# Sliding-window attention and a token/channel mixer on one Trainium2 core: one pool of eight PSUM banks, one burst of scores per pair of heads, sinks' values by the whole array

## Chip, cores, metric

The kernel runs on one core of one Trainium2 chip. The metric is the device time of one execution in microseconds (us); lower is better. The engines are named as in the profile: PE (matmuls; PEld are its weight loads), DVE (vector), ACT (scalar and exp), POOL (which here mostly issues DMAs that cast), SP (which issues DMAs).

## The reference

```python
# q, k, v: (4 batches, 8 heads, 768 rows, 64); n_sink = 4, window = 128
scores = (q @ k.T) / 8
keep = (pos_k < 4) | ((pos_q - pos_k >= 0) & (pos_q - pos_k < 128))
a = softmax(where(keep, scores, -1e9))
x = (a @ v)                         # laid out as (4, 768, 512)
h = relu(x.T @ w_tok1) @ w_tok2     # 768 -> 256 -> 768, over the rows
u = x + h.T
out = u + relu(u @ w_ch1) @ w_ch2   # 512 -> 1536 -> 512, over the channels
```

Each query row thus sees the 128 keys up to its own and the first four keys of the sequence, the sinks.

## The kernel before

**Tiles.** The 8 heads of a batch are taken as 4 pairs, 16 pairs in all (0 to 3 are batch 0). Scores are made transposed: keys on the partitions, queries along the free dimension, the two heads `i` of a pair beside each other. A key tile `kt` of 128 keys needs only query tiles `kt` and `kt + 1`, so a pair has six key tiles of 256 queries (128 for the last); two key tiles are a group `g`, and a pair has three groups. ACT takes exp of a group out of PSUM into `pT` (L588). Then either DVE multiplies by a mask of ones and zeros (L596), or, in some groups of batch 0, PE has added -32768 before the scores (`masked`, units named `m` in FIRST_BATCH). `v_aug` is v with a column of ones, so that the value matmuls also give the sum of exps; DVE takes the reciprocal and multiplies (L656 to L700) into `x_sb`.

**Sinks.** Query tiles 2 to 5 see the sinks outside their window. `score_sinks` (L610) takes two pairs at once: four matmuls of 512 columns, 32 rows for each head of each pair, and one exp into `pT_sink`. `v_sink` holds the sinks' values in the matching rows and zeros elsewhere: two copies of four rows for each pair (`sink_rows`, L727). In batch 0 and for pair 15, `pv` (L635) adds them by one whole-array matmul of 130 columns for each query tile. From pair 4 to 14, `sink_values` (L676) does it with eight matmuls of 64 rows, and `values` (L711) follows with eleven whole-array matmuls of 65 columns for each head.

**Order.** All engines run an order that the program works out while it is built: a planner (class `Plan`, L265) with a cost for each operation places units of PE work and hands evictions to ACT or DVE, whichever is sooner. It hands out PSUM banks too: a unit starts on PE only when the banks that it needs have been read. Three lists written out by hand steer it. FIRST_BATCH orders the units of batch 0's attention and token mixer. From then on the channel mixer is the main list: for each batch 24 units `v1` (four matmuls of 384 columns each, relu by ACT or DVE) and then 24 units `out` (three matmuls of 512 columns, four units into one bank). Attention and token mixer of the next batches are the side list, and MERGED says for each side unit after how many main units it is placed. LOADS orders the loads on POOL's queue. Units that use only a part of the array are gathered into a `burst`, since a change between whole-array and partial work costs PE time (SWITCH in the planner).

**PSUM** has eight banks of 128 x 512 fp32: two pairs of banks with the tag `sc` for scores (and the q and k transposes of pairs 5 to 7), four single banks `mx` for the rest. A pair of banks that held transposes is cleared by a memset (L521), because exp reads places that no score was written to, and exp of a stale number times a mask of zero may not be zero.

**A pair from 4 on** has two bursts: the transposes of the next pair's q and k if PE does them (pairs 5 to 7; from pair 8 on DMAs transpose), the scores of group 0 by halves (K = 64, 128 keys), and the sink values of the pair before; then, later, groups 1 and 2 by eighths (32 keys by 160 queries, eight parts of the array side by side), and for every other pair the sinks' scores.

**Start.** SP issues the fp32 loads of q and k of pairs 0 and 1, four small loads of the first batch's sinks into `v_sink_f` (L213) and the loads of pairs 2 and 3. POOL copies `v_sink_f` to `v_sink` (one copy), and then issues v1, v2, w_tok1 (`T0`) and so on.

Of the kernel before, what the change touches and what calls it, by code (L numbers as in the profile page):

```python
# [9 lines left out]
FP32 = mybir.dt.float32  # L10
# [6 lines left out]
def kernel(  # L17
# [35 lines left out]
    )  # L53
    FIRST_BATCH = (
        "q0 k0 m00 s00 m01 s01 q1 m02 k1 s02 m11 x1 s11 m10 q2 s10 o01 m12 k2 s12 o00 m21 q3 s21 s20 k3 o11 "
        "s22 x3 o10 m31 s30 s31 o20 h0 m32 o21 s32 h1 o30 o31 y01 u00 h2 u10 u11 t00 h3 u20 t01 t11 y30 t10 "
        "u21 t20 t30 u31 t31 t21"
    )
    LOADS = (
        "v1 v2 T0 v3 A0 k4 q4 q5 C0 v4 k5 C1 v5 q6 C2 k6 C3 k7 q7 D0 q8 v6 k8 D1 D2 D3 v7 k9 q9 q10 v8 k10 "  # L60
        "k11 q11 v9 v10 k12 k13 q12 q13 v11 v12 k14 q14 v13 k15 q15 v14 v15"
# [16 lines left out]
    TAGS = {"sc": 2, "mx": 4}  # L78

    given = {}  # L80

    sc = [psum.tile([P, 2, 2, 4, D], FP32, name=f"ps_sc{n}", tag=f"sc{n}", bufs=1) for n in range(TAGS["sc"])]

    def bank(tag, *shape, dtype=FP32, slot=None):

        n = given[tag].pop(0) if slot is None else slot
        if tag == "sc":
            return sc[n]
        return psum.tile([P, *shape], dtype, name=f"ps_{tag}", tag=f"{tag}{n}", bufs=1)
# [69 lines left out]

    ones = singles.tile([P, 4 * P], BF16)  # L160
    in_order(nc.vector.memset(ones, 1.0))  # L161

    def keep_warm(n, slot):
        ps = bank("mx", 4 * P, slot=slot)
        for _ in range(n):
            mm(ps, ones[:, 0:P], ones, start=True, stop=True)

    keep_warm(7, 0)


# [4 lines left out]
    MASKED = -32768.0  # L175
    mask_add = singles.tile([P, 4, 2, P], BF16)
# [993 lines left out]
```

## Time and profile before

| | |
|---|---|
| three runs | 199.54, 199.54, 199.82 us; median 199.54 |
| the profiled execution | 199.51 us, of which the span from first to last instruction is 197.7 |
| granted clock of PE | 1.00 throughout |

In a row of the order of time stand the start in us, the length, the engine, the line, the operation, output and input with their shapes, and how many of them in a row were merged; in brackets the idle time before it and what ended it. In a row of the groups stand busy time in all, mean ns of one, and the idle time of the engine before them. Matmuls are pipelined: the length of a row contains the latency of the last one, and the distance of two starts is what PE spent. Nearly all matmuls have the line of a helper, L134, so they are told apart by tiles and shapes: `ps_sc<-qT,kT` are scores, `ps_mx<-qT,kT` sink scores, `ps_mx<-v_sink,pT_sink` sink values, `ps_mx<-v_aug,pT` values, `ps_mx<-uT,w_ch` v1 units and `ps_mx<-w_ch,v1T` out units.

### The profile page before, as it was taken

To read this page: it belongs to the slowest core of one execution; us is meant where nothing else is said; L and a number is where in the kernel's file an instruction comes from. 1 tells how busy PE (TensorE), PEld (TensorE's weight loads), DVE (VectorE), ACT (ScalarE), POOL (GpSimd) and SP (SyncE) were. 2 spreads that over 40 slices of the span, in tenths; PEclk is the share of its full clock that TensorE was granted. 3 is DMA by queue.
4 is the path that set the end of the run, shared out by engine and by line. 5 is a ranking of instruction groups with operands and counts; after the bars stand their busy time and mean duration, and the time that the engine had idled before them with its cause. 6 is when DMAs were issued, how large, how long until landed. Compare 5 with 4: busy or idle time off the path is not lost.

```text
span 197.7 us, 5262 instructions
## 1 busy us (share of the span) xinstructions
PE 190.7 (96%) x2251; PEld 114.5 (58%) x2251; DVE 102.6 (52%) x218; ACT 106.6 (54%) x188; POOL 67.6 (34%) x86
## 2 busy tenths in 40 slices
PE   6798999999999999999999999999999999999993
PEld 1345895566764655565556755566656645564453
DVE  4697775878774656340756886443352631001222
ACT  4798657987717027867735753868701006772000
POOL 6099797789538933159450000000000000000000
PEclk9999999999999999999999999999999999999999
DMA  6999999999999999999999997100002391000223
GB/s 193 281 268 150 169 176 177 188 179 169 183 154 162 133 179 206 156 183 137 148 156 143 209 175 182 56 0 5 0 0 109 84 230 57 0 3 0 106 106 106
DMA packets 92359, 26.30 MB, mean 133 GB/s; under 512 B 82352, under 2 KB 89392, under 8 KB 92336
## 3 DMA queue, kind: packets, MB, share of 16 engines
q0 software_dynamic: 67232, 11.80, 81.5%
q1 hardware_dynamic: 25104, 14.17, 34.6%
q8 instruction: 17, 0.28, 0.6%
q14 instruction: 6, 0.05, 0.1%
HBM read 26.75 MB, written 6.29 MB: 167 GB/s over the span
## 4 chain that ended last, share of the span: by engine, by line
PE 88%; DMA 7%; POOL 1%; DVE 1%; SPq 0%; issue 0%; POOLq 0%
PE ps_mx L134 82%; PE ps_sc L134 4%; DMA w_tok<-in_moe_w_tok_dram 4%; DMA v_sink_f<-in_v_dram 3%; POOL v_aug L127 1%; PE ps_mx L137 1%; PE ps_sc L503 1%; PE ps_mx L475 1%; SPq L213 0%; POOL v_sink L143 0%; PE ps_mx L487 0%; DVE v_sink_f L209 0%; DVE mask_add L178 0%; DVE ones L161 0%; DVE v_aug L195 0%
## 5 line engine op out<-in xcount | busy, mean ns | idle before, releaser
L134 PE MATMUL ps_mx<-w_ch,v1T 128*128 128x512 bf16 (+2 forms) x312 | 67.2, 363 | 0.0
L134 PE MATMUL ps_mx<-uT,w_ch 128*128 128x384 bf16 x384 | 66.8, 326 | 0.0
L147 ACT ACTIVATE v1T<-ps_mx 128x384 bf16<-128x384 f32 x82 | 40.3, 492 | 29.6 <-PE ps_mx L134 18.1
L588 ACT ACTIVATE pT<-ps_sc 128x1024 bf16<-128x1024 f32 (+1 forms) x48 | 44.2, 952 | 16.0 <-PE ps_sc L134 15.7
L134 PEld LDWEIGHTS <-w_ch 128*128 128x128 bf16 x384 | 36.0, 98 | 23.5 <-issue 0.9
L134 PEld LDWEIGHTS <-v1T 128*128 128x128 bf16 x312 | 28.3, 98 | 26.8 <-issue 0.2
L1006 DVE TENSOR_TENSOR o_sb<-ps_mx,u_sb 128x512 f32<-128x512 f32 x23 | 15.9, 690 | 36.9 <-PE ps_mx L134 31.1
L119 POOL DMA_DIRECT2D q_bf<-in_q_dram x24 | 19.8, 830 | 15.2 <-DMA v_aug<-in_v_dram 6.8
L134 PEld LDWEIGHTS <-w_tok 128*128 128x128 bf16 x240 | 19.5, 98 | 5.2 <-issue 0.4
L119 POOL DMA_DIRECT2D k_bf<-in_k_dram x24 | 19.8, 832 | 5.3 <-DMA v_aug<-in_v_dram 2.2
L805 DVE TENSOR_TENSOR u_sb<-ps_mx,x_sb 128x512 bf16<-128x512 f32 (+1 forms) x24 | 15.4, 655 | 8.2 <-PE ps_mx L134 8.0
L127 POOL DMA_DIRECT2D v_aug<-in_v_dram x16 | 16.5, 1038 | 7.3 <-DMA w_ch<-in_moe_w_ch_dram 2.2
L149 DVE TENSOR_SCALAR v1T<-ps_mx 128x384 bf16<-128x384 f32 x14 | 7.6, 550 | 18.9 <-PE ps_mx L134 18.8
L134 PEld LDWEIGHTS <-pT 128*128 128x128 bf16 x352 | 14.7, 98 | 4.0 <-issue 1.0
L134 PE MATMUL ps_mx<-v_aug,pT 128*128 128x65 bf16 x352 | 16.1, 193 | 0.0
L596 DVE TENSOR_TENSOR pT<-pT,mask_main 128x768 bf16<-128x768 bf16 (+1 forms) x25 | 14.8, 617 | 2.0 <-ACT pT L588 1.9
L134 PE MATMUL ps_mx<-h1T,w_tok 128*128 128x256 bf16 (+1 forms) x120 | 14.2, 251 | 0.0
L134 PE MATMUL ps_sc<-qT,kT 64*32 64x160 bf16 (+3 forms) x480 | 14.0, 232 | 0.2 <-ACT kT L141 0.2
L147 ACT ACTIVATE h1T<-ps_mx 128x512 bf16<-128x512 f32 (+1 forms) x9 | 4.5, 505 | 16.1 <-PE ps_mx L134 16.1
L134 PEld LDWEIGHTS <-kT 64*32 64x32 bf16 (+1 forms) x512 | 7.1, 91 | 9.1 <-issue 7.8
L134 PE MATMUL ps_mx<-x_sb,w_tok 128*128 128x256 bf16 (+1 forms) x120 | 12.2, 251 | 0.1
L698 DVE TENSOR_TENSOR x_sb<-ps_mx,recip 128x384 bf16<-128x384 f32 x22 | 11.8, 547 | 0.4
(64 smaller groups left out, 120.2 us busy)
## 6 DMA issues: line engine op xcount, KB each, us to landing
out_dram<-o_sb SPq DMA_DIRECT2D x23, 256.0 KB, 4.8
v_aug<-in_v_dram POOLq DMA_DIRECT2D x16, 192.0 KB, 8.6
w_ch<-in_moe_w_ch_dram POOLq DMA_DIRECT2D x8, 384.0 KB, 7.9
k_bf<-in_k_dram POOLq DMA_DIRECT2D x24, 96.0 KB, 7.7
q_bf<-in_q_dram POOLq DMA_DIRECT2D x24, 96.0 KB, 8.4
q_f<-in_q_dram SPq DMA_DIRECT2D x4, 384.0 KB, 5.7
k_f<-in_k_dram SPq DMA_DIRECT2D x4, 384.0 KB, 5.2
w_tok<-in_moe_w_tok_dram POOLq DMA_DIRECT2D x2, 384.0 KB, 8.0
```

The source lines that it names most:

```text
L119: in_order(nc.gpsimd.dma_start(out=out[:, h], in_=rows[:, h]))
L127: in_order(nc.gpsimd.dma_start(out=v_aug.rearrange("p i t d -> p (i t) d")[:, :, 0:D], in_=v[b].rearrange("h s d -> (h s) d")[2 * hp * S:2 ...
L134: in_order(nc.tensor.matmul(*args, skip_group_check=True, **kwargs))
L137: in_order(nc.tensor.transpose(out, in_, ident))
L147: in_order(nc.scalar.activation(out, in_, AF.Relu))
L149: in_order(nc.vector.tensor_scalar_max(out=out, in0=in_, scalar1=0.0))
L475: in_order(nc.tensor.transpose(outs[x][columns], rows_by_columns[rows, columns], ident[rows, rows]))
L588: in_order(nc.scalar.activation(part(tiles["pT", p][:, :, ds(2 * g, 2)]), of_keys(tiles["ps_s", p, g])[:, :, 0:width(g)], AF.Exp, scale=scale,
L596: in_order(nc.vector.tensor_tensor(out=pt, in0=pt, in1=m, op=ALU.mult))
L698: in_order(nc.vector.tensor_tensor(out=x_sb[b][:, :, ds((2 * hp + i) * D, D)], in0=tiles["ps_o", p, i][:, :, 0:D], in1=tiles["recip", p, i ...
L805: in_order(nc.vector.tensor_tensor(out=u_part(b, g, s0, n), in0=tiles["ps_u", b, g, s0], in1=x_sb[b][:, s0:s0 + n, c0:c0 + cn], op=ALU.add,))
L1006: in_order(nc.vector.tensor_tensor(out=o_sb.rearrange("p (g c) -> p g c", g=2), in1=u_rows(b, st), in0=tiles["ps_out", b, st].rearrange("p ...
```

## The change

The eight banks become slices of one tensor and one pool, `mx`; scores take any two that are free (`two_banks`). All scores are made by eighths, those of batch 0 too. The sinks' scores of a pair stand in its third group, in the 128 columns that its last key tile leaves unused, 32 rows for each of the query tiles 2 to 5, so that the third exp is 1024 wide and `score_sinks` with its exp goes. From pair 4 on, a pair has one burst with all three groups and the sinks, which needs six banks at once; transposes and u transposes are bursts by themselves. `v_sink` gets zeros everywhere but in four rows for each query tile, and `pv` uses whole-array matmuls of 65 columns for each head and query tile for all pairs; `sink_values` and `values` go. A pair's sink rows take four copies in place of two. The mask holds 0 and about 3.3e38 and is applied by minimum, so nothing is cleared. The first sinks are loaded by four DMAs on ACT's queue at the very start and copied by four POOL operations. MERGED, FIRST_BATCH and LOADS are new orders.

```diff
     MERGED = (
-        "1/0 0/2 2/3 3/7 7/10 4/14 6/15 5/17 8/18 10/19 9/20 11/21 12/22 15/24 13/24 16/24 14/24 17/24 18/25 "
...
+        "0/0 1/2 2/4 6/12 5/16 3/16 4/22 7/24 8/27 10/32 11/32 9/33 19/36 17/36 18/38 12/40 21/40 22/40 13/41 "
+        "15/41 23/41 14/41 25/42 24/42 26/43 27/45 16/45 20/55 28/62 29/71 30/71 31/74 32/74 33/80 38/80 "
+        "40/81 34/82 39/83 43/83 42/83 35/83 36/83 37/83 44/84 47/86 46/86 45/86 41/88 48/94 50/108 52/109 "
+        "53/110 51/112 49/115 54/123 58/123 59/128 55/128 61/128 56/128 60/130 62/130 57/132 63/132 65/135 "
+        "64/135 66/135"
     )
     FIRST_BATCH = (
...
+        "q0 k0 m00 m02 s00 m01 s02 q1 s01 k1 m10 m12 s10 m11 s12 m21 q2 k2 s11 o01 o00 s21 m20 s20 q3 k3 s22 "
+        "o10 m32 s30 o11 m31 s32 s31 o20 o21 h0 h1 o30 o31 h2 u11 u10 u00 h3 u20 y01 y30 t00 u31 t10 t01 t20 "
+        "t11 t30 t31 u21 t21"
...
     LOADS = (
-        "v1 v2 T0 v3 A0 k4 q4 q5 C0 v4 k5 C1 v5 q6 C2 k6 C3 k7 q7 D0 q8 v6 k8 D1 D2 D3 v7 k9 q9 q10 v8 k10 "
...
+        "v1 v2 T0 v3 A0 k4 q4 C0 q5 C1 v4 C2 k5 q6 k6 C3 D0 D1 D2 D3 v5 k7 q7 v6 v7 v8 k8 q8 k9 q9 q10 k10 "
...
-    TAGS = {"sc": 2, "mx": 4}
+    TAGS = {"sc": 0, "mx": 8}
...
+    banks = psum.tile([P, TAGS["mx"], 8 * D], FP32, name="banks")
...
+    def two_banks():
+        a, b = sorted(given["mx"].pop(0) for _ in range(2))
+        return banks[:, a:b + 1:b - a]
...
+    v_sink0 = singles.tile([P, NHP, NT - 2, 2, D1], BF16, name="v_sink")
+    v_sink_f = singles.tile([P, NHP, 2, D], FP32)
+    for c in range(NT - 2):
+        in_order(nc.scalar.dma_start(
+            out=v_sink_f[ds(ODD * c, n_sink)].rearrange("s p i d -> s (p i) d"),
+            in_=v[0, :, 0:n_sink].rearrange("h s d -> s h d"),
+        ))
...
-    keep_warm(7, 0)
+    for n in range(TAGS["mx"]):
+        mm(banks[:, n], ones[:, 0:P], ones, start=True, stop=True)
...
+    in_order(nc.vector.memset(v_sink0, 0.0))
...
     def transposed(p):
-            ps = turned_bank(p)
+            ps = shaped_pair(two_banks(), 2 * NT * D).rearrange("d x (n j p) -> d x n j p", n=2, j=NT)
...
-        then.append(cleared(p, then))
...
     def scores(p, g):
         def by_eighths(ps):
             for k in range(2):
                 for c in range(4):
                     a = 4 * (2 * g + k) + c
-                    nq = min(P + ODD, S - ODD * a)
+                    nq = min(P + ODD, S - ODD * a) if a else 2 * P
...
+        def of_sinks(ps):
+            for c in range(NT - 2):
+                for i in range(2):
+                    rows = ds(D * i, D)
+                    mm(
+                        ps[ds(ODD * c, ODD), i, 3 * P:], tiles["kT", p][rows, 0:ODD],
+                        tiles["qT", p][rows, ts(2 + c, P)], start=True, stop=True,
+                    )
...
-            in_order(nc.vector.tensor_tensor(out=pt, in0=pt, in1=m, op=ALU.mult))
+            in_order(nc.vector.tensor_tensor(out=pt, in0=pt, in1=m, op=ALU.min))
...
-        x.cost, x.fn, x.deps = {"ACT": 190.0 + 1.5 * width(g)}, exp, [("pv", p - NPT)] if p >= NPT else []
+        x.cost, x.fn, x.deps = {"ACT": 960.0}, exp, [("pv", p - NPT)] if p >= NPT else []
...
-        return piece((190, 165, 125)[g] if eighths else width(g) * 0.47, run, deps, {} if by_pe else {"sc": [[x]]}, then, [("s", p)])
+        return piece((185, 155, 185)[g], run, deps, {} if by_pe else {"mx": [[x], [x]]}, then, [("s", p)])
...
     def pv(p, half):
-                if qt >= 2:
-                    mm(
-                        ps_o[:, qq].rearrange("p i d -> p (i d)"), tiles["pT_sink", p][:, ts(qt - 2, P)],
-                        vsk.rearrange("p i d -> p (i d)"), start=True, stop=False,
-                    )
                 for i in range(2):
+                    if qt >= 2:
+                        mm(ps_o[:, qq, i], pT[:, i, NT - 1, 1], vsk[:, qt - 2, i], start=True, stop=False)
...
     def sink_rows(p):
+        def copies(e):
+            for c in range(NT - 2):
+                copy(e, v_sinks[p % NHP][ODD * c:ODD * c + n_sink, c], vs[p][0:n_sink, :, 0])
...
     def attention_and_tokens():
+            units.append(burst(*[scores(p, g) for g in range(NT // 2)]))
+            units[-1].then.append(sink_rows(p))
+            if p + 1 < BY_DMA:
+                units.append(burst(transposed(p + 1)))
             if p > first:
-                units += [values(p - 1, i) for i in range(2)]
+                units += [pv(p - 1, half) for half in range(2)]
...
+    def first_sinks(e, c):
+        rows = slice(ODD * c, ODD * c + n_sink)
+        copy(e, v_sink0[rows, :, c, :, 0:D], v_sink_f[rows])
+
+    v_sink = [Op({"POOL": 600.0}, lambda e, c=c: first_sinks(e, c), [landed(6000.0)]) for c in range(NT - 2)]
...
-                    out=m[:, i], in0=a, scalar1=-1.0 / MASKED, scalar2=1.0, op0=ALU.mult, op1=ALU.add,
+                    out=m[:, i], in0=a, scalar1=-MASKED, scalar2=KEPT, op0=ALU.add, op1=ALU.mult,
```

In the new MERGED the side units of pair 4 + n stand in the order scores, transposes of the next pair (pairs 5 to 7), values of the pair before, and a token-mixer group behind pairs 2 and 0 of a batch: scores of pairs 4 to 15 are units 2, 4, 8, 17, 20, 28, 31, 38, 41, 48, 51 and 58, transposes of pairs 5 to 7 are units 3, 5 and 9, and the u transposes of batch 1 are units 16 and 27.

More of the change, by code (lines that the diff above doesn't have):

```diff
@@ L544, in masked @@
         deps = [done["tk", 0]] if p == 0 else []
-        done["mask", p, g] = unit(width(g) * 0.84, run, deps, {"sc": [[x]]})
+        done["mask", p, g] = unit(width(g) * 0.84, run, deps, {"mx": [[x], [x]]})
         return done["mask", p, g]
@@ L711, in values @@
-    def values(p, i):
-        def run():
-            pT, v_aug = tiles["pT", p], vs[p]
-            for qt in range(NT):
-                out = tiles["ps_o", p, i][:, qt]
-                mm(out, pT[:, i, qt, 0], v_aug[:, i, qt], start=False, stop=(qt == 0))
-                if qt >= 1:
-                    mm(out, pT[:, i, qt - 1, 1], v_aug[:, i, qt - 1], start=False, stop=True)
-        deps = [done["v", p]] + [done["p", p, g] for g in range(NT // 2)]
-        deps.append(("sv", p))
-        op = unit(305, run, deps, {}, [done["r", p, i], done["x", p, i]])
+        deps += [done["p", p, g] for g in range(NT // 2)]
@@ L724, in values @@
+        op = unit(560 if half else 375, run, deps, {"mx": [[r, n]]}, [r, n])
         done.setdefault(("pv", p), []).append(op)
@@ L913, in first_attention, with tokens @@
         return [[made[name] for name in names]]
+    def tokens(b, g):
+        units = [mix_h(b, g, 0, NTOK)] + [mix_u(b, g, st, 2) for st in range(0, NT, 2)]
+        if (b, g) in U_BY_DMA:
+            transfer_u(b, g)
+        else:
+            units.append(burst(turned_u(b, g)))
+        return units
     def attention_and_tokens():
```

226 lines of the change are left out of this document (43 added, 183 removed), and 4 rows, old and new, of the table MERGED.

## The prediction

> **What bounds the kernel now.** First the page's busy times, then a table of stretches.
>
> ```profile
> span 197.7 us, 5262 instructions
> ...
> PE 190.7 (96%) x2251; PEld 114.5 (58%) x2251; DVE 102.6 (52%) x218; ACT 106.6 (54%) x188; POOL 67.6 (34%) x86
> ...
> PEclk9999999999999999999999999999999999999999
> ```
>
> ```profile
> 15.00:20.00 5.00, 4.23 (x87) 2.66 (x88) 3.83 (x10) 4.29 (x6) 5.00 (x7) 1.00 1.61 152
> 20.00:25.00 5.00, 5.00 (x99) 4.66 (x100) 3.90 (x11) 3.13 (x6) 3.57 (x5) 1.00 2.04 168
> ...
> 170.00:194.67 24.67, 24.63 (x152) 13.67 (x150) 4.18 (x8) 7.33 (x15) 0.00 (x0) 1.00 0.14 54
> ```
>
> In the table the first number behind the stretch is its length, then come busy PE, PEld, DVE, ACT and POOL. From 20 us to 194.67 us PE is never idle, at full clock. But busy can hide pipeline waits, so I read the order of time on PE, start to start, around one pair of heads:
>
> ```profile
> 96.25 2.75 PE L134 MATMUL ps_mx<-w_ch,v1T 128*128 128x512 bf16 x12
> 98.94 0.39 PE L134 MATMUL ps_sc<-qT,kT 64*128 64x256 bf16 x4
> 99.17 0.28 PE L134 MATMUL ps_mx<-v_sink,pT_sink 64*128 64x65 bf16 x8
> 99.39 2.76 PE L134 MATMUL ps_mx<-w_ch,v1T 128*128 128x512 bf16 x12
> 101.99 0.50 PE L134 MATMUL ps_mx<-v_aug,pT 128*128 128x65 bf16 x11
> 102.32 2.10 PE L134 MATMUL ps_mx<-w_ch,v1T 128*128 128x512 bf16 x9
> 104.26 0.50 PE L134 MATMUL ps_mx<-v_aug,pT 128*128 128x65 bf16 x11
> 104.69 0.44 PE L134 MATMUL ps_sc<-qT,kT 64*32 64x160 bf16 x32
> 105.06 0.39 PE L134 MATMUL ps_mx<-w_ch,v1T 128*128 128x512 bf16 x1
> ```
>
> Twelve 512-column matmuls take 101.99 − 99.39 = 2.60 us, 217 ns each, 2.4 columns a ns: no bank or operand is waited for. The twelve from 96.25 thus end at 98.85, and the scores begin at 98.94: about 0.09 us goes each time the array changes between whole-array and partial-array work. So the second part of the run, 175 us long, is a sum of PE work, and any matmul time saved there shortens the run one for one. The first 20 us have gaps and are another matter.
>
> **Steady part (pairs 4 to 15): what goes.** The first burst of a pair (four scores by halves, eight sink-value matmuls) costs 99.39 − 98.85 = 0.54 us. The second burst follows eleven value matmuls of 0.33 us (102.32 − 101.99) that end at 104.59; it costs 105.06 − 104.59 = 0.47. On every other pair it also has four 512-column sink scores:
>
> ```profile
> 123.10 0.44 PE L134 MATMUL ps_sc<-qT,kT 64*32 64x160 bf16 x32
> 123.38 0.40 PE L134 MATMUL ps_mx<-qT,kT 64*32 64x512 bf16 x4
> 123.71 4.72 PE L134 MATMUL ps_mx<-uT,w_ch 128*128 128x384 bf16 x28
> ```
>
> That is 0.09 + 0.61 = 0.70. Before, over twelve pairs: 11 x 0.54 + 0.32 (pair 4 has no sink values to carry) + 6 x 0.47 + 6 x 0.70 = 13.3 us of bursts, and 22 x 0.33 = 7.3 us of values for pairs 4 to 14. Pair 15 already runs `pv` with four 130-column sinks; eight of 65 stream the same columns, so it comes out even, at the 0.9 us worked out below. Together 21.5.
>
> **What comes.** One burst: 48 scores of 32 keys and eight sink scores, all on 64-by-32 parts of the array. The 32 of groups 1 and 2 start within 0.28 us (123.38 − 123.10), four rounds of eight, 0.07 each for at most 160 columns. Group 0 is two more rounds, one with 256 columns in its first part: 0.07 + 0.11 = 0.18. The sinks' round of 128 columns is 0.055. With a change of mode on each side: 0.09 + 0.18 + 0.28 + 0.06 + 0.09 = 0.70, twelve times 8.4 us. No row shows group 0 in eighths or sinks of 128 columns: below, group 0 costs a plain 0.14; above, the 0.23 that by halves takes (99.17 − 98.94); the sinks between 0.04 and 0.11 (two rounds). That makes 0.64 to 0.81 a burst.
>
> Values are now 12 + 18 whole-array matmuls of 65 columns. Eleven in 0.33 to 0.34 us is 30 to 31 ns each, their weight loads hidden, so 30 x 0.0305 = 0.915 us a pair (0.90 to 0.93), twelve times 11.0. The sinks on the whole array cost more than on halves (0.915 against 0.67 plus the 0.22 of the first burst), and the change pays this back with the mode changes and the half-array scores.
>
> The transposes leave the first burst:
>
> ```profile
> 41.25 0.35 PE L503 MATMUL ps_sc<-ident,q_bf 64*128 64x64 bf16 x12
> ...
> 41.61 0.38 PE L134 MATMUL ps_sc<-qT,kT 64*128 64x256 bf16 x4
> ...
> 57.76 0.58 PE L475 MATMUL ps_mx<-ident,u_sb 64*64 64x64 bf16 x48
> 58.27 4.71 PE L134 MATMUL ps_mx<-w_ch,v1T 128*128 128x512 bf16 x21
> ```
>
> They cost 0.36 per pair as before. In the new MERGED units 5 and 3 (pairs 6 and 5) stand together at 16, unit 9 (pair 7) alone at 33, and both u transposes (units 27 and 16, 0.5 each as before) together at 45: three extra mode visits of 0.18, +0.55. After: 8.4 + 11.0 + 0.55 = 19.95, against 21.5. **Gain 1.5 us**; with the bounds above (burst −0.7 to +1.3, values −0.2 to +0.2) between 0.0 and 2.4. About all of it is mode changes: 24 bursts become 12 and three visits, nine times 0.18 = 1.6.
>
> **ACT and DVE**, off this path as long as banks come free in time:
>
> ```profile
> L588 ACT ACTIVATE pT<-ps_sc 128x1024 bf16<-128x1024 f32 x32 | 32.4, 1024 | 15.4 <-PE ps_sc L134 15.2
> L588 ACT ACTIVATE pT<-ps_sc 128x768 bf16<-128x768 f32 x16 | 12.9, 809 | 0.6 <-PE ps_sc L134 0.5
> L141 ACT ACTIVATE v_sink<-v_aug 4x65 bf16<-4x65 bf16 x20 | 5.0, 252 | 4.5 <-DMA v_aug<-in_v_dram 4.2
> L627 ACT ACTIVATE pT_sink<-ps_mx 128x512 bf16<-128x512 f32 x8 | 4.8, 599 | 0.0
> L596 DVE TENSOR_TENSOR pT<-pT,mask_main 128x768 bf16<-128x768 bf16 (+1 forms) x25 | 14.8, 617 | 2.0 <-ACT pT L588 1.9
> ...
> L149 DVE TENSOR_SCALAR v1T<-ps_mx 128x384 bf16<-128x384 f32 x14 | 7.6, 550 | 18.9 <-PE ps_mx L134 18.8
> ```
>
> The third exp grows from 0.81 to 1.02 (16 x 0.215 = +3.4 us) and the sink exps go (−4.8). The sink copies, two a pair, become four: at least 24 x 0.25 = +6 us. Both engines are about half idle, which covers it; without cover each set of four copies is 1.0 us in front of an eviction. The mask keeps its shape and its engine; minimum for multiply is taken at nothing (no row has minimum; half its 0.62 us more would be 0.3 a mask, on DVE's idle half). The bank-clearing memsets go.
>
> **Banks.** A burst now needs six of eight at once. The exp of the burst at 98.94 shows the lag:
>
> ```profile
> 99.37 1.02 ACT L588 ACTIVATE pT<-ps_sc 128x1024 bf16<-128x1024 f32 x1 [1.16 <-PE ps_sc L134]
> ```
>
> The first two banks are free 1.45 us after the first score. PE finishes the burst at 0.6, and two v1 units (four 384-column matmuls, 0.65 each) fill the other two banks until 1.9: slack 0.45 us. By MERGED five bursts fall among v1 units (4, 22, 55, 62, 112, each batch having 24 v1 and then 24 out units); seven among out units, where four units share a bank. The costs in the planner put an exp at 0.96 where the trace has 1.02; three of them are 0.18 late, at five bursts 0.9 at most. I take 0.3 lost here, from 0 to 0.9.
>
> **The first 20 us.**
>
> ```profile
> 3.56 1.14 POOL L127 DMA_DIRECT2D v_aug<-in_v_dram  x1
> 9.62 0.61 POOL L143 CAST v_sink<-v_sink_f 128x520 bf16<-128x520 f32 x1 [4.93 <-DMA v_sink_f<-in_v_dram]
> 10.19 2.02 POOL L127 DMA_DIRECT2D v_aug<-in_v_dram  x2
> 12.19 0.84 POOL L152 DMA_DIRECT2D w_tok<-in_moe_w_tok_dram  x1
> ...
> 20.00 0.67 PEld L134 LDWEIGHTS <-w_tok 128*128 128x128 bf16 x12 [0.20 <-DMA w_tok<-in_moe_w_tok_dram]
> ```
>
> ```profile
> 9.65 0.49 ACT L141 ACTIVATE kT<-ps_mx 128x384 bf16<-128x384 bf16 x1 [0.66 <-PE ps_mx L487]
> ...
> 15.32 0.49 ACT L141 ACTIVATE qT<-ps_mx 128x384 bf16<-128x384 bf16 x1 [0.46 <-PE ps_mx L487]
> ...
> 19.33 1.94 ACT L588 ACTIVATE pT<-ps_sc 128x1024 bf16<-128x1024 f32 x2 [0.32 <-PE ps_sc L134]
> ```
>
> ```profile
> 1.46 0.48 DVE L178 MEMSET mask_add<- 128x512 uint32 x1
> ...
> 4.95 0.56 DVE L143 CAST k_bf<-k_f 128x768 bf16<-128x768 f32 x1 [1.74 <-DMA k_f<-in_k_dram]
> ```
>
> The first sinks' DMAs move from SP, behind four large loads, to ACT's queue at its start. One POOL copy becomes four (0.6 each at 512 columns, +1.8 us); behind them on POOL wait v1, v2 and w_tok1, whose landing released the token mixer at 20.00. If the sinks land before 4.70 (end of the row at 3.56), the copies end at 7.1 and w_tok1 is issued 3 us sooner; if they land at 9.6 as now, 1.8 us later. I take early, a queue of its own, and give little for it: PE lacked only 0.20 us there, ACT's three gaps (1.4 us in all) are what an earlier start could fill, and earlier v loads share the DMA engines with the last q and k. Between −1.4 and +1.8, taken −0.3. The Trainium skill ("DMA: Bandwidth & Descriptors", Queues, rings and completion order) has each DMA engine go round its queue rows packet by packet, so by it the sinks no longer stand behind SP's loads and the early case holds; the row at 9.62 shows only the late landing on SP's own queue. The zeroing of the larger v_sink (1040 words at 0.48 per 512, 1.0 us) fits in DVE's 1.74 idle before 4.95; one more warm-up matmul ends at about 4.9, when the first transpose begins.
>
> **Sum.** −1.5 + 0.3 − 0.3 = −1.5 on 199.51 (the profiled execution's own time, 1.8 more than its span and 0.03 below the median of 199.54): **198.0 us**; its own range, from ends that seldom fall together, 196.4 to 199.6. About 0.2% (0.4 us) is what these runs can tell from no change.
>
> **Rivals.** *A, evictions fall behind a burst (slower).* ACT gets three exps and four copies in a row, 4.1 us; PE at 0.65 a unit needs six evictions meanwhile; DVE with three masks (about 1.9) has room for four of 0.55. Two come late, about 1.0 us of PE waiting at each of the five v1-stage bursts: +4.9 in place of the 0.3: 202.6. It decides from 0.36 us a burst on, where 5 x 0.36 eats the 1.8 of the other two terms. For it: ACT in order, only two banks left; against: the present order has the same exps on four other banks without a wait, and DVE's idle. The Trainium skill ("TensorEngine Tiling (Array Packing)", PSUM Bottleneck) warns that packing speeds PE up but not the emptying of PSUM; no row here shows such a wait. Chance 0.20. *B, waits between slices.* All banks are one tensor now; if a wait is kept for banks lying between the two of a pair, PE stands for an exp each burst: 199.5 − 1.8 + 12 x 1.0, about 210. For it: the old pairs of banks were a tensor each; against: each matmul names one bank. Chance 0.03. *C, the start is late* (sinks land late, as they do now, w_tok1 +1.8): 199.5 − 1.5 + 0.3 + 1.8 = 200.1; 0.08. *D, the start fills ACT's gaps* (−1.4): 196.9; for it the sinks' own queue, against it the loads that then share; 0.11. *My sum*: 0.58.
>
> **How the numbers follow.** Faster: most of the sum (0.52) and D (0.11), 0.63. Same: the weak ends of the sum (0.05), of A (0.03) and of C (0.02), 0.10. Slower: A 0.17, B 0.03, C 0.06, the sum 0.01, 0.27. The range, 196.2 to 201.0, holds the sum, C and D and a mild A; it leaves out a full A and B, some 0.18.
>
> **What would show it.** Steps right: a burst of 56 small matmuls in about 0.6 us between whole-array neighbours, values 30 ns apart, no PE idle after 20 us, 217 ns for 512 columns next to bursts. Wrong: PE or its weight loads waiting for an exp or a v1 eviction behind a burst (A, B), w_tok1 issued after 12.2 us (C), values above 31 ns, or scores of group 0 above 0.23.

## The result, and the profile after

The changed kernel takes 217.81 us (median of 6 runs, 217.38 to 219.32); the kernel before, on the same chip, 199.66 (6 runs, 199.19 to 200.35). The ratio is 1.092 (95% interval 1.088 to 1.096): 18.2 us slower, where 198.0 was predicted. The profiled execution took 217.38 us with a span of 215.5. The page of the changed kernel:

```profile
span 215.5 us, 6116 instructions
...
PE 191.2 (89%) x2635; PEld 119.4 (55%) x2658; DVE 108.6 (50%) x239; ACT 108.9 (51%) x179; POOL 70.4 (33%) x89
...
q8 instruction: 21, 0.34, 0.6%
```

PE is busy for 191.2 us, against 190.7 before: it has no more work, it waits. Where, the table of stretches says (length, then busy PE, PEld, DVE, ACT and POOL, the granted clock, DMA share and GB/s):

```profile
10.00:15.00 5.00, 3.13 (x71) 1.53 (x71) 2.43 (x6) 3.52 (x5) 5.00 (x7) 0.97 1.98 217
15.00:20.00 5.00, 4.32 (x112) 2.84 (x108) 3.00 (x7) 3.63 (x5) 4.66 (x7) 0.69 1.80 189
20.00:25.00 5.00, 3.28 (x120) 2.32 (x121) 3.60 (x8) 2.67 (x5) 3.36 (x5) 1.00 1.86 175
...
40.00:60.00 20.00, 16.18 (x213) 9.72 (x213) 8.29 (x16) 13.02 (x22) 14.00 (x17) 1.00 2.02 163
60.00:80.00 20.00, 17.93 (x298) 11.53 (x301) 14.99 (x34) 9.50 (x14) 14.96 (x18) 1.00 1.89 154
```

Before, PE was busy without a gap from 20 us to 194.67. Now it loses 3.8 of the 20 us behind 40 and 2.1 of the next 20, and its mean granted clock from 15 to 20 us is 0.69. The waits of PE by what ended them (us in total, times, longest):

```profile
PE banks L146 <- ACT pT L576: 13.5, 16, 1.5
PE banks L146 <- DVE kT L155: 1.7, 1, 1.7
...
PE banks L491 <- ACT pT L576: 0.9, 2, 0.5
```

L576 is the exp, L155 the eviction of k's transposes by DVE. Both read two banks in one instruction. 16.1 us of PE's time end with one of them. A stretch in order of time shows whom they hold:

```profile
55.21 0.82 PE L146 MATMUL banks<-uT,w_ch 128*128 128x384 bf16 x4
55.40 1.02 ACT L576 ACTIVATE pT<-banks 128x1024 bf16<-128x1024 f32 x1 [0.25 <-PE banks L146]
...
56.47 0.81 PE L146 MATMUL banks<-uT,w_ch 128*128 128x384 bf16 x4 [0.44 <-ACT pT L576]
...
57.32 1.02 ACT L576 ACTIVATE pT<-banks 128x1024 bf16<-128x1024 f32 x1 [0.90 <-DVE pT L584]
...
58.40 0.19 PE L146 MATMUL banks<-v_sink,pT 128*128 128x65 bf16 x1 [1.11 <-ACT pT L576]
```

At 56.47 a v1 unit starts when the exp of 55.40 ends. A v1 unit has nothing to do with an exp: its operands are u and weights. At 58.40 the values of the pair before wait for the next exp of the new pair. Read alone, this could be a shortage of banks (the prediction's rival A) or waits between slices (its rival B). The program's bank numbers speak for B: 24 pieces of PE work wait for a reader of a pair without sharing a bank or an operand with it, and each of the 24 writes a bank whose number lies between the two of that pair. `banks[:, a:b + 1:b - a]` names banks a and b, but the order is kept as if it named a to b. These waits stand in the program as it is built, so they come from how the accesses of a tensor are tracked there, and not from the chip. The other direction stands in it too: 21 reads of a pair wait for PE work that writes only a bank between the two. The runs below test it.

### The profile page after: what moved, and what is told of

Read it like the earlier page. It is cut to its first block, busy times and chain, and to the rows that moved or that the text cites. A ratio compares the mean times of both kernels' runs of the same rounds, so it can differ in the third digit from the quotient of the medians.

```text
span 215.5 us, 6116 instructions
## 1 busy us (share of the span) xinstructions
PE 191.2 (89%) x2635; PEld 119.4 (55%) x2658; DVE 108.6 (50%) x239; ACT 108.9 (51%) x179; POOL 70.4 (33%) x89
## 4 chain that ended last, share of the span: by engine, by line
PE 73%; ACT 8%; DMA 8%; DVE 6%; issue 2%; SPq 0%; ACTq 0%; DVEq 0%
PE banks L146 72%; ACT pT L576 8%; DMA v_aug<-in_v_dram 4%; DMA w_ch<-in_moe_w_ch_dram 3%; DMA k_f<-in_k_dram 2%; DVE kT L155 1%; ACT qT L153 1%; DVE o_sb L874 1%; PE banks L507 1%; DVE v_sink L155 1%; DVE k_bf L155 1%; DVE v1T L161 1%; DVE x_sb L619 1%; PE banks L479 1%; DVE qT L155 1%
## 5 line engine op out<-in xcount | busy, mean ns | idle before, releaser
L146 PE MATMUL banks<-uT,w_ch 128*128 128x384 bf16 x384 | 66.0, 326 | 5.2 <-ACT pT L576 3.5
L146 PE MATMUL banks<-w_ch,v1T 128*128 128x512 bf16 (+2 forms) x293 | 64.8, 362 | 5.1 <-ACT pT L576 3.7
L576 ACT ACTIVATE pT<-banks 128x1024 bf16<-128x1024 f32 x48 | 47.6, 1023 | 21.2 <-PE banks L146 14.1
L159 ACT ACTIVATE v1T<-banks 128x384 bf16<-128x384 f32 x82 | 40.0, 491 | 28.4 <-PE banks L146 16.2
L874 DVE TENSOR_TENSOR o_sb<-banks,u_sb 128x512 f32<-128x512 f32 x23 | 15.9, 690 | 39.9 <-PE banks L146 34.2
L146 PE MATMUL banks<-v_aug,pT 128*128 128x65 bf16 x352 | 18.9, 196 | 1.1 <-ACT pT L576 1.1
L712 DVE TENSOR_TENSOR u_sb<-banks,x_sb 128x512 bf16<-128x512 f32 (+1 forms) x24 | 14.8, 651 | 6.1 <-PE banks L146 5.9
L619 DVE TENSOR_TENSOR x_sb<-banks,recip 128x384 bf16<-128x384 f32 x32 | 17.5, 554 | 0.7
L146 PE MATMUL banks<-qT,kT 64*32 64x160 bf16 (+5 forms) x896 | 13.4, 231 | 3.5 <-ACT pT L576 3.3
L146 PE MATMUL banks<-v_sink,pT 128*128 128x65 bf16 x128 | 14.8, 197 | 1.7 <-ACT pT L576 1.7
```

Source lines behind the costliest of these rows:

```text
L146: in_order(nc.tensor.matmul(*args, skip_group_check=True, **kwargs))
L159: in_order(nc.scalar.activation(out, in_, AF.Relu))
L576: in_order(nc.scalar.activation(tiles["pT", p][:, :, ds(2 * g, 2)].rearrange("p i k n q -> p i (k n q)"), tiles["ps_s", p, g], AF.Exp, sca ...
L619: in_order(nc.vector.tensor_tensor(out=x_sb[b][:, ts(half, QH), ts(hp, 2 * D)].rearrange("p t (i d) -> p t i d", i=2), in0=tiles["ps_o", p ...
L712: in_order(nc.vector.tensor_tensor(out=u_part(b, g, s0, n), in0=tiles["ps_u", b, g, s0], in1=x_sb[b][:, s0:s0 + n, c0:c0 + cn], op=ALU.add,))
L874: in_order(nc.vector.tensor_tensor(out=o_sb.rearrange("p (g c) -> p g c", g=2), in1=u_rows(b, st), in0=tiles["ps_out", b, st].rearrange("p ...
```

## Experiments

Ratios are to runs of the kernel before on the same chip, with their 95% interval.

**Two reads.** The changed kernel, same banks and order, each read of a pair cut in two:

```diff
-            in_order(nc.scalar.activation(
-                tiles["pT", p][:, :, ds(2 * g, 2)].rearrange("p i k n q -> p i (k n q)"), tiles["ps_s", p, g], AF.Exp,
+            for i in range(2):
+                in_order(nc.scalar.activation(
+                    tiles["pT", p][:, i, ds(2 * g, 2)].rearrange("p k n q -> p (k n q)"), tiles["ps_s", p, g][:, i],
...
-            copy(e, to if parts == 1 else to[:, part], tiles["ps_" + name, p] if parts == 1 else tiles["ps_" + name, p][part])
+            for x in range(2) if parts == 1 else [part]:
+                copy(e, to[:, x], tiles["ps_" + name, p][:, x] if parts == 1 else tiles["ps_" + name, p][x])
```

> The changed kernel with the same banks and the same order of PE's work; only the readers of a two-bank pair are cut in two (each exp, and the evictions of the q and k transposes of pairs 5 to 7), one instruction per bank, so that none reads with a stride over the banks that lie between. Waits between slices (the span of banks a to b taken as one range): PE's rows that wait for an exp (13.5 + 0.9 us) and for a kT copy (1.7 us) go, 16.1 of the 217.4, and with them most of the clock's dip at 15 to 20 us: 197 to 202 us, though ACT pays two exps of about 0.6 us for one of 1.02. Real shortage of banks (six of eight in one burst): banks stay held as long or longer, so PE waits as before: 214 to 220 us. A late start that has nothing to do with these waits (the 1.79 us memset, POOL's four copies): the first v1 unit still begins near 35 us and not near 30, 202 to 205 us.

203.89 us (203.16 to 204.53), ratio 1.021 (1.017 to 1.025): 13.9 us of the 18.2 are gone. The time lies in the third of the expected ranges: the waits between slices go, and a late start stays. All waits of PE of 0.3 us and more in it:

```profile
PE banks L146 <- issue: 2.2, 1, 2.2
PE banks L146 <- DVE ones L183: 1.5, 1, 1.5
PE banks L492 <- DVE k_bf L155: 1.3, 2, 0.8
PE banks L146 <- DMA v_aug<-in_v_dram: 1.0, 1, 1.0
PE banks L492 <- ACT pT L578: 0.3, 1, 0.3
PE banks L146 <- DVE qT L155: 0.3, 1, 0.3
```

All of these lie in the first 25 us. With the same eight banks and six of them in each burst, no v1 unit and no value waits for an exp any more, though ACT holds the banks longer (0.61 us for each half, 1.02 for both together before). So rival A, real shortage, falls. What is left is at the start: the first v1 unit begins at 33.88 us, and at 29.35 in the kernel before.

**Neighbours, and far pairs.** The same exps over two banks, but the choice of the banks is edited: always two neighbours, or the lowest and the highest free one.

```diff
-                given[tag] = [n for _, n in self.slots(tag)[:len(banks)]]
+                given[tag] = self.place(tag, banks, t)
...
+            def pairs_in(left, k):
+                if k == 0:
+                    return []
+                for a in sorted(left, reverse=True):
+                    if a + 1 in left:
+                        rest = pairs_in(left - {a, a + 1}, k - 1)
+                        if rest is not None:
+                            return [(a, a + 1)] + rest
+                return None
```

For far pairs, the loop is this instead:

```diff
+                a, b = min(left), max(left)
+                rest = pairs_in(left - {a, b}, k - 1)
+                return None if rest is None else [(a, b)] + rest
```

> The changed kernel with its single exps over two banks, but the two banks of a pair always neighbours (the search for free banks waits until two neighbours are free), so that no bank lies between them. Waits between slices: no PE row waits for an exp after 20 us, 198 to 203 us (the order stays the one that was found for free pairs, and a burst may have to wait for neighbours). Real shortage of banks: choosing neighbours makes the shortage worse, 217 us or more.

> As the run with neighbours, by the same search, but each pair takes the lowest and the highest free bank, so that the banks between them are as many as can be (19 PE pieces then write a bank that lies inside a pair that is still being read; 24 in the changed kernel, none with neighbours). Waits between slices: 201 plus about 19/24 of 16 us, 209 to 219 us, with PE's rows waiting for exps again. Real shortage of banks: which free bank is taken is of no matter, so the time of the changed kernel or up to 3 us less, as in the run with two reads.

Neighbours: 205.46 us, ratio 1.030 (1.026 to 1.035), above the range: the search for neighbours costs PE 0.95 us of idle time between 40 and 60 us, and the start has waits that do not come from banks (below). Far pairs: 225.76, ratio 1.129 (1.123 to 1.136), also above its range, 8 us slower than the changed kernel, though fewer pieces of PE work wait in this way (19 against 24) and only a few more reads of pairs do (25 against 21); with neighbours the program has none of either. The number of waits is thus no price list. The waits of PE, and of the page's groups the exps, in the run with far pairs:

```profile
PE banks L146 <- ACT pT L614: 13.4, 15, 1.2
PE banks L146 <- DVE kT L155: 3.8, 2, 1.9
```

```profile
L614 ACT ACTIVATE pT<-banks 128x1024 bf16<-128x1024 f32 x48 | 47.6, 1024 | 31.8 <-PE banks L146 28.7
```

PE's own waits are little longer than in the changed kernel, but the exps now stand idle for 28.7 us until a PE matmul ends (14.1 in the changed kernel). That the wait works both ways shows best at the transposes of pairs 5 and 6:

```profile
55.43 0.34 PE L545 MATMUL banks<-ident,k_bf 64*128 64x64 bf16 x12
...
57.66 1.46 PE L146 MATMUL banks<-uT,w_ch 128*128 128x384 bf16 x8 [1.89 <-DVE kT L155]
...
59.16 0.81 ACT L153 ACTIVATE qT<-banks 128x768 bf16<-128x768 bf16 x1 [2.54 <-PE banks L146]
```

Two v1 units wait for the first pair's kT copy, and the second pair's qT copy, whose transposes were done at 55.8, then waits for these v1 units. Where the 8 us come from was not settled wait by wait: in the profiled executions 6.1 of the 9.6 us of longer span lie before the first v1 unit (41.10 against 35.02).

**The kernel before, with one tensor, and then with its pairs apart.** If the cause is the read over other banks, it must work without any other part of the change.

```diff
-    sc = [psum.tile([P, 2, 2, 4, D], FP32, name=f"ps_sc{n}", tag=f"sc{n}", bufs=1) for n in range(TAGS["sc"])]
+    banks = psum.tile([P, 8, 8 * D], FP32, name="banks")
+    SC, MX = ((0, 1), (2, 3)), (4, 5, 6, 7)
+    sc = [banks[:, a:b + 1:b - a].rearrange("p x (n b c) -> p x n b c", n=2, b=4) for a, b in SC]
...
-        return psum.tile([P, *shape], dtype, name=f"ps_{tag}", tag=f"{tag}{n}", bufs=1)
+        t = banks[:, MX[n]] if dtype == FP32 else banks[:, MX[n]].bitcast(dtype)
```

For the pairs apart, one line differs:

```diff
-    SC, MX = ((0, 1), (2, 3)), (4, 5, 6, 7)
+    SC, MX = ((0, 3), (4, 7)), (1, 2, 5, 6)
```

> The kernel before with one edit: its eight PSUM banks are one tensor, as in the changed kernel, the two pairs of the scores on neighbouring banks (0 and 1, 2 and 3) and the four single banks behind them (4 to 7). If one tensor for all banks costs by itself (waits between any of its slices), slower, above 202 us; if only a pair read over other banks does, the time of the kernel before, 199 to 200 us.

> The run before this one with other bank numbers only: the scores' pairs are banks 0 and 3, and 4 and 7, the single banks 1, 2, 5 and 6, so that each single bank lies inside a pair. Same instructions, same order, same shortage of banks. Waits between slices: 39 PE pieces get a wait for a reader of a pair round their bank; at the changed kernel's (217.8 - 203.9) / 24 = 0.58 us each that is 22 us, so 215 to 228 us. Without such waits, or if the stride itself is of no matter: 199 to 200 us.

One tensor with neighbours: 199.23 us, ratio 1.002 (0.999 to 1.005), no difference. The same program with other bank numbers: 230.83, ratio 1.162 (1.154 to 1.169), 31.6 us slower and above the expected range. In the run with pairs apart, PE's waits and one of them in order of time:

```profile
PE banks L145 <- ACT pT L599: 17.5, 24, 1.2
PE banks L145 <- DVE banks L532: 4.2, 2, 2.3
PE banks L498 <- ACT pT L599: 3.2, 5, 1.6
```

```profile
62.58 0.49 PE L145 MATMUL banks<-v_aug,pT 128*128 128x65 bf16 x11 [1.95 <-DVE banks L532]
```

L532 is the memset that clears a pair of banks, here 4 and 7: eleven value matmuls into bank 6 stand 1.95 us for it. In the program with pairs apart 39 pieces of PE work wait for a pair round their bank and 34 reads of pairs for PE work inside them; with neighbours none do. An exp over two banks takes 1.02 us in both kernels, so the stride itself does not slow ACT. This settles the main cause: one tensor is harmless, neighbours are harmless, and a strided read or write over other banks holds every user of those banks.

**The start: zeroing later, scores by halves, both.** All three on the run with two reads. First the ones of `v_aug` ahead of the zeroing of `v_sink`; then batch 0's scores as in the kernel before.

```diff
-    in_order(nc.vector.memset(v_sink0, 0.0))
     for n in range(NV):
         in_order(nc.vector.memset(v_buf[n][:, :, :, D:D1], 1.0))
+    in_order(nc.vector.memset(v_sink0, 0.0))
```

```diff
-            by_eighths(tiles["ps_s", p, g])
+            (by_halves if p < NHP else by_eighths)(tiles["ps_s", p, g])
```

> The run with two reads, with one instruction moved on DVE: the zeroing of v_sink (1.79 us) behind the six memsets of v_aug's ones instead of ahead of them, so that the load of the first v (v0) is issued at 3.6 us and not at 4.49. If the 4.5 us by which the first v1 unit is late there (33.88 against 29.35) come from the loads at the start: v0 lands about 0.9 us sooner, PE's 1.0 us wait for v_aug at 15.3 goes, 202.5 to 203.3 us. If the sinks and the loads of q and k that now run ahead hold v0 up anyway, it lands near 15.3 as before: no change, 203.5 to 204.3. The 2.17 us wait at 19.8, for which the profile shows nothing waited for, stays in either case.

> The run with two reads, with the scores of pairs 0 to 3 cut as in the kernel before: four instructions of 128 keys per group instead of 16 (24 in the last group's burst with the sinks), 36 matmuls and as many weight loads less per pair. Theory of PE's instruction stream: in the run with two reads PE stops for 2.17 us at 19.8 us in the middle of a row of values whose operands it already used, and so does the run with neighbours at the same instruction (2.07 us); the queue of instruction loads has 17 packets before and 21 after. If PE outran its instructions there, with fewer of them the wait goes, and with it the clock of 0.68 at 20 to 25 us: about 3 us less, 200.3 to 201.5. If it waited for data (a load of v or w_tok), the wait stays at about 21.9 us and the time at 203 to 204.5.

> Both of the last two edits on the run with two reads. If the late start is v0's load and PE's instructions and nothing else, the first v1 unit begins within 0.7 us of the kernel before (29.35) and the time is 199.0 to 200.5; if the rest of the loss is in the steady part (ACT's two exps, the burst), the first v1 unit begins there too but the time stays above 201.5.

Zeroing later alone: 203.78 us, ratio 1.022 (1.019 to 1.024), no gain. v0's load is issued at 3.6 us, but it takes 13.4 us to land in place of 10.8, and PE waits 2.06 us for it; the wait of 2.17 us that was to stay is 0.5 there, behind this one. By halves: 200.46, ratio 1.007 (1.005 to 1.009); it is 1.2 us over the kernel before on its chip where the run with two reads is 4.3, so 3.1 us are gone, and the first v1 unit begins at 30.95 us. Both: 199.64, ratio 1.002 (0.999 to 1.005), level with the kernel before. Its profiled execution took 206.71 us and does not tell where the first v1 unit begins in the others; with the same edits and zeroing by words (below) it is 30.70, later than the 0.7 us that was allowed. So the cut of the first twelve groups of scores into 32 keys, which the prediction had not costed, is most of the late start. What it cost in the run with two reads is a wait for which the profile names nothing, amid the values of one pair, at an instruction that waits for no semaphore in the program:

```profile
19.54 0.23 PE L146 MATMUL banks<-v_aug,pT 128*128 128x65 bf16 x2
21.94 0.21 PE L146 MATMUL banks<-v_sink,pT 128*128 128x65 bf16 x1 [2.17 <-issue]
```

```profile
20.00:25.00 5.00, 3.06 (x68) 1.99 (x68) 1.91 (x4) 1.71 (x5) 3.13 (x5) 0.68 1.87 174
```

The stop costs twice: behind it PE runs at a lower clock, 0.68 in the mean of these 5 us. The run with neighbours has three of them:

```profile
15.46 0.38 PE L146 MATMUL banks<-v_aug,pT 128*128 128x65 bf16 x7 [0.42 <-issue]
...
21.93 0.21 PE L146 MATMUL banks<-v_sink,pT 128*128 128x65 bf16 x1 [2.07 <-issue]
...
28.28 0.20 PE L146 MATMUL banks<-v_aug,pT 128*128 128x65 bf16 x1 [0.69 <-issue]
```

Counted in the rows of PE and PEld by their start, they stand behind 447, 703 and 958 rows, 256 and 255 apart (the expectation of the run with masks cut fine, below, counts a little otherwise), and 6.4 us apart in time; the one in the run with two reads behind 703, those in the run with zeroing later behind 701 and 956. On the page, the queue of instruction loads has 17 packets before and 21 after, for 4,502 and 5,316 matmuls and weight loads: about 256 to a packet.

**Is it PE's instructions?** The run by halves with the warm-up cut fine, and then the run by halves with masks and scores cut fine in place of the warm-up:

```diff
-        mm(banks[:, n], ones[:, 0:P], ones, start=True, stop=True)
+        for x in range(16):
+            mm(banks[:, n, ds(32 * x, 32)], ones[:, 0:P], ones[:, ds(32 * x, 32)], start=True, stop=True)
```

> The run with the scores of pairs 0 to 3 by halves, with the eight warm-up matmuls of 512 columns (on ones, over before 5 us) cut into 128 of 32 columns: 120 matmuls and 120 weight loads more, about what the cut by halves had taken out by 20 us, and nothing else. The warm-up then takes 128 x about 30 ns = 3.9 us and not 3.4. If PE outruns its instructions in the first 20 us, a wait with nothing waited for comes back at 15 to 24 us, of 0.5 to 2.5 us, with a dip of the clock: 201.5 to 204. If that wait hung on data or on the cut of the scores, none: 200.3 to 201.3.

201.14 us (199.85 to 201.80), ratio 1.010 (1.007 to 1.014), and no such wait above 0.2 us in the profile: by its own terms the theory had fallen. But its profile is of the fastest of the six executions; two of the others have a mean granted clock of 0.991, as runs with stops have, and may have stopped. And that run had moved the boundaries of the blocks and not filled the time between two of them. Its successor does that. Cut this way, the kernel no longer computes the right attention for batch 0 (apparently not all of the added masks stay in the sums), so it serves for its times alone.

```diff
-                mm(
-                    ps[:, i, 0:width(g)], ident,
-                    mask_adds[g == 0].rearrange("p k n q -> p (k n q)")[:, 0:width(g)], start=True, stop=False,
-                )
+                for x in range(width(g) // D):
+                    mm(
+                        ps[:, i, ts(x, D)], ident,
+                        mask_adds[g == 0].rearrange("p k n q -> p (k n q)")[:, ts(x, D)], start=True, stop=False,
+                    )
...
-                for i in range(2):
-                    mm(
-                        ps[:, i, ds(2 * k * P, nq * P)], tiles["kT", p][ds(D * i, D), ts(kt, P)],
-                        tiles["qT", p][ds(D * i, D), kt * P:(kt + nq) * P], start=not by_pe, stop=True,
-                    )
+                for x in range(nq):
+                    for i in range(2):
+                        mm(
+                            ps[:, i, ds((2 * k + x) * P, P)], tiles["kT", p][ds(D * i, D), ts(kt, P)],
+                            tiles["qT", p][ds(D * i, D), ts(kt + x, P)], start=not by_pe, stop=True,
+                        )
```

> The run with the scores of pairs 0 to 3 by halves, with more PE instructions for the same columns between 6 and 24 us: each mask matmul of 512 or 384 columns is cut into 8 or 6 of 64, each score of 256 into two of 128; 168 matmuls and 168 weight loads more. Theory of instruction blocks: the stops without a reason stood after 446, 702 and 952 of PE's rows (matmuls and weight loads) in the run with neighbours, 703 in the run with two reads, 700 and 955 with v first, 948 with far pairs, so 256 rows are one block, and a block takes about 6.4 us to come while the loads of the start fill the DMA engines. The run by halves needs 6.4 and 6.6 us for its two blocks from 13.0 us on and never stops; the run with the cut warm-up only moved the boundaries and needed 8.8 and 6.8. Here PE does about 48 rows a us in place of 26, 256 in 5.3 us: stops of 0.4 to 2 us come back after about 446, 702 and 952 rows, and the time is 201.3 to 204. If the cut of the scores itself or late data made the stop, none: 199.9 to 201.

203.98 us, ratio 1.025 (1.020 to 1.029), and the stops are back behind 447 and 703 rows, the same counts in a program that is cut otherwise, 6.5 us apart, with the clock behind them:

```profile
15.17 0.19 PE L492 MATMUL banks<-ident,q_bf 64*128 64x64 bf16 x1 [0.49 <-issue]
21.64 0.27 PE L146 MATMUL banks<-v_aug,pT 128*128 128x65 bf16 x2 [2.37 <-issue]
```

```profile
20.00:25.00 5.00, 3.36 (x63) 3.02 (x64) 1.79 (x5) 1.66 (x4) 3.55 (x6) 0.66 1.85 176
```

The traces also have the packets of the queue of instruction loads, 16,384 bytes each. Each of these stops ends 1.5 to 1.8 us behind the end of one (1.3 and 1.6 in the run with zeroing later):

| run | packet, from and to (us) | PE goes on at | behind the packet's end |
|---|---|---|---|
| neighbours | 12.86, 13.75 | 15.46 | 1.71 |
| neighbours | 19.48, 20.43 | 21.93 | 1.50 |
| neighbours | 25.88, 26.81 | 28.28 | 1.47 |
| two reads | 19.50, 20.46 | 21.94 | 1.48 |
| masks | 12.39, 13.39 | 15.17 | 1.78 |
| masks | 19.19, 20.14 | 21.64 | 1.50 |

So in the loaded start PE gets a block of 256 instructions about every 6.4 us, and stops when it uses them faster. The load of the DMA engines has a part in it: in the run with neighbours the next packet begins 4.0 us after PE has passed row 447 (15.46 and 19.48), and at row 4,287, with the DMA engines idle, no later than PE passes it (138.69 and 138.21). What fills the time between a packet's end and PE's next row, no row shows.

**Towards a version under both kernels.** Three more runs on the run with both start edits: `v_sink` zeroed as words; then also its first casts moved from POOL to DVE; or, with words, the sinks' loads back on SP's queue and the casts spread over three engines.

```diff
-    v_sink0 = singles.tile([P, NHP, NT - 2, 2, D1], BF16, name="v_sink")
+    v_sink_w = singles.tile([P, NHP * (NT - 2) * D1], FP32, name="v_sink")
+    v_sink0 = v_sink_w.bitcast(BF16).rearrange("p (a c i d) -> p a c i d", a=NHP, c=NT - 2, i=2)
...
-    in_order(nc.vector.memset(v_sink0, 0.0))
+    in_order(nc.vector.memset(v_sink_w, 0.0))
```

```diff
-    v_sink = [Op({"POOL": 600.0}, lambda e, c=c: first_sinks(e, c), [landed(6000.0)]) for c in range(NT - 2)]
+    v_sink = [Op({"DVE": 360.0}, lambda e, c=c: first_sinks(e, c), [landed(6000.0)]) for c in range(NT - 2)]
```

```diff
-        in_order(nc.scalar.dma_start(
+        in_order(nc.sync.dma_start(
...
-    v_sink = [Op({"POOL": 600.0}, lambda e, c=c: first_sinks(e, c), [landed(6000.0)]) for c in range(NT - 2)]
+    v_sink = [Op(({"POOL": 600.0}, {"DVE": 420.0}, {"ACT": 560.0}, {"DVE": 420.0})[c], lambda e, c=c: first_sinks(e, c), [landed(9600.0)]) for c in range(NT - 2)]
```

> The run with both start edits (zeroing moved, scores of pairs 0 to 3 by halves), with v_sink zeroed as 1040 words of four bytes in place of 2080 of two. If a DVE memset goes by its elements (512 words took 0.48 us), it takes 1.0 us and not 1.79; it ended at 4.4 and k_bf's cast waited for its DMA anyway, so the time stays within 0.5 us of that run's 199.6.

> The run with words, with the four casts of the sinks' values moved from POOL (0.84 us each, 5.6 to 9.0 us) to DVE. In the runs so far DVE's rows are slow just while POOL does these casts: the two masks of 512 take 0.89 us and not 0.49, and k1's cast 0.99 and not 0.56, so that the second k is turned at 10.6 to 11.1 us and not at 9.27. If the two engines hold each other up, these rows go back to 0.49 and 0.56, the first v1 unit begins 0.5 to 1.3 us sooner and the time is 198.2 to 199.3, under the kernel before. If instead the loads of v1, v2 and w_tok, which POOL now issues 3.4 us sooner, push the second q and k back, it is 199.6 to 201.5.

> The run with words, with the sinks' loads back on SP's queue behind the loads of pairs 0 and 1, as in the kernel before, and their four casts spread: one on POOL, two on DVE, one on ACT. It tries for a version under both kernels: the first v1 unit at 29.3 to 30.0 us as in the kernel before and the steady part as short as in the last runs (167.6 us from there to the end, against 168.35) would make 198.4 to 199.2. If the casts at 9.6 us stand in front of qT and kT copies instead, the first v1 unit comes at 30.5 or later and the time is 199.7 to 201.

Words: 200.10 us, ratio 1.005 (1.002 to 1.008); the memset takes 0.93 us and not 1.79, and nothing follows, as expected. Casts on DVE: 201.54, 1.016 (1.011 to 1.020), the time of the second case but not its reason. The second k lands at 9.08 us, before the 9.58 of the run with words; its cast begins at 10.64 in place of 9.60, behind two sink casts and two qT copies on DVE, and PE waits 1.98 us for it. Nor do the masks' rows go back: they take 1.02 and 0.90 us, now while POOL issues loads. Sinks on SP: 200.54, 1.006 (1.004 to 1.009), first v1 unit at 30.97 us, the second case. No run came out under the kernel before.

## The prediction, step by step

**The step that failed** is the term for the banks: "I take 0.3 lost here, from 0 to 0.9", and with it rival B, which had the right mechanism with a chance of 0.03 and was put aside because "each matmul names one bank". The matmul does, but its partner, the exp, names two with a stride, and the order is kept for all banks in that span. Rival B's price (one wait of 1.0 us a burst, "about 210") was too small as well: PE's wait rows add up to 16.1 us, values and pieces of the start wait too, the exps wait for PE in turn, and the clock falls. The price in the time is 217.8 − 203.9 = 13.9 us.

**Rival A** (evictions behind a burst) fell: with the reads cut in two, PE waits for no eviction after 25 us.

**The steady sum** was right in kind. From the first v1 unit to the end of the span, the run by halves takes 198.5 − 30.95 = 167.55 us and the kernel before 197.7 − 29.35 = 168.35: a gain of 0.8 where 1.5 was forecast (167.52 and 167.61 in the runs with two reads and with words; 168.43 in the kernel before with one tensor). The bursts in that run, in order of time on PE:

```profile
66.25 0.35 PE L146 MATMUL banks<-v_aug,pT 128*128 128x65 bf16 x6
...
67.11 0.22 PE L146 MATMUL banks<-v_aug,pT 128*128 128x65 bf16 x2
...
77.40 4.71 PE L146 MATMUL banks<-uT,w_ch 128*128 128x384 bf16 x28
82.04 0.78 PE L146 MATMUL banks<-qT,kT 64*32 64x256 bf16 x56
82.75 4.72 PE L146 MATMUL banks<-uT,w_ch 128*128 128x384 bf16 x28
```

The 28 v1 matmuls (0.163 us each, three quarters of the 217 ns of 512 columns) end at 81.96; the burst thus costs 82.75 − 81.96 = 0.79 us, at the upper end of 0.64 to 0.81 and 0.09 above the 0.70 that was taken: 12 x 0.09 = 1.1 us of the gain, more than the 0.7 that is missing. The values (28 matmuls from 66.25 to 67.11 and two more, 0.92 us) are the 0.915 of the text. That the change saves mode changes and loses little to the sinks on the whole array held.

**The start** was taken at −0.3. The first v1 unit came 5.7 us late in the changed kernel (35.02 against 29.35), 4.5 of it with no wait between slices. Right: the sinks landed early, though w_tok1 was issued only 1.0 us sooner (11.19 against 12.19) and not 3. Mis-sized: the zeroing of `v_sink` takes 1.79 us and not 1.0, since it runs over 2,080 elements of two bytes, and not over words; POOL's casts take 0.80 each and not 0.6. Left out: the scores of batch 0 by eighths, whose columns cost about the same but whose instructions do not (3.1 us). The late v_sink zeroing cost 0.4 to 0.8 us (200.46 against 200.10 and 199.64 with it moved), hardly more than the noise, and only once that was out of the way. In the run with words some 1.3 us of a late start remains (30.70 against 29.35). POOL's work beside DVE has a part in it: on DVE in the changed kernel,

```profile
2.33 1.79 DVE L211 MEMSET v_sink<- 128x2080 bf16 x1 [0.38 <-issue]
...
5.91 0.89 DVE L992 TENSOR_SCALAR mask_main<-mask_add 128x512 bf16<-128x512 bf16 x2
```

and on POOL beside it,

```profile
5.63 3.37 POOL L155 CAST v_sink<-v_sink_f 4x512 bf16<-4x512 f32 x4
```

the pair of masks takes 0.89 us where it took 0.49 in the kernel before, when POOL was idle. It takes 0.49 again with the sinks on SP, when POOL is idle too, and 1.02 with the casts on DVE, when POOL issues loads: it is POOL at work, and not its casts alone. How the 1.3 us split between this and the loads' order was not settled.

**What would show it wrong** was named rightly: PE waiting for an exp was the first line to look at, and it was there.

## What to carry to other kernels

When buffers become slices of one tensor, look at every access that strides over slices: it may be ordered against all that lies between, on both sides, so give such pairs neighbours or one instruction for each part. A v1 unit waiting for an exp is the sign: a wait for work that shares no operand. And cutting matmuls finer at equal columns is not free where PE must be fed with instructions in a phase full of DMAs.

## What the hardware showed unexpectedly

In the first 29 us PE stops for 0.4 to 2.4 us at boundaries of 256 instructions when it does them in less than about 6.4 us, and goes on 1.3 to 1.8 us behind the end of the next packet of instructions; with 6.4 to 6.6 us a block (the profiled execution of the run by halves) it does not stop. The Trainium skill ("Runtime: NRT & Kernel Launch", Instruction fetch mechanics) gives the same 256 instructions for a block but has its cost "mostly hidden"; here it was up to 2.4 us.

A stop of 2.1 to 2.4 us at the start is followed by a mean granted clock of 0.66 to 0.68 over 5 us. In the traces' clock records this is one stretch of 3.41 us at half clock: from 21.84 us in the run with two reads, where PE goes on at 21.94. The run with zeroing later has one from 17.48 us, behind its wait of 2.06 us for v0, so a wait for data is followed by one too. The changed kernel has one from 14.66 us, behind several shorter waits; the kernel before and the run by halves have none. In the run with two reads, PE's 3.06 us of work from 21.94 to 25 us, all at half clock, contain up to about 1.5 us of slowdown (an estimate, half of the 3.06), beside the stop's 2.17.
